# Scan and expert block in one kernel: masked logs as the moving operand, and one weight shift of four units on another engine

## The chip, the cores and the metric

One core of one Trainium2 chip runs the whole program. The metric is the device time of one execution in microseconds (us). The median of three runs of the kernel before is 324.29 us, the lowest 323.87 us. The execution that was profiled took 324.25 us, and its trace covers a span of 322.6 us.

## The reference, cut to what matters

A decayed scan over 4 batches, 8 heads and 768 positions, in chunks, and behind it a two-layer block over all 3072 tokens:

```
log_a = np.log(np.clip(a, 1e-06, 1.0))
cum = np.cumsum(la, axis=-1)
L = np.exp(cum[:, :, :, None] - cum[:, :, None, :]) * causal
y[:, :, sl] = einsum(CB * L, xc) + einsum(Cc, state) * decay_to_i
state = decay_full * state + np.sum(Bx, axis=2)
...
h = x @ w_in
g = h - np.tanh(h)
return (g @ w_out).astype(np.float32)
```

The weights `w_in` (256 x 2048) and `w_out` (2048 x 256) arrive as 64-bit floats. The chip gets them as pairs of 32-bit words, and has to make 32-bit floats of them itself.

## The kernel before, in words

**Scan.** The 768 positions of a batch are cut into chunks of Q = 112, and the chunks of the four batches take turns: numbers 0 to 3 are the first chunk of each batch, 4 to 7 the second, and so on to 27. A chunk stands in 128 partitions, of which the first N = 16 hold the carried state and the other 112 the positions. For each chunk the kernel makes `att` (the products of B and C, on PE into PSUM), `lt` (the exponentials of sums of logs, by ACT), their product (DVE), a triangular cut of it (POOL, except in the first four chunks), and `y` (PE). ACT copies of `y` into rows 0 to 15 of a later chunk's `x` hand on the state, `z0` and `z1` doing this for the first four chunks. There is one buffer for `att` from chunk 4 on, so the next `att` may be written only when DVE has read the one before.

**First four chunks.** Their exponents are made by `first_tile`. For each half of the heads (i = 0, 1), `fn_k` (L443) lets POOL write four 128x128 tiles `lm`, one for each head: the log of partition j, where j lies behind column m, and zero elsewhere. `fn_f` first adds the table `never` through the unit matrix `eye` (L448), which puts a large negative number where the causal mask is zero, and then multiplies (L451) each head's `lm` as weights with the triangle `upto` moving, 112 columns a head. ACT takes the exponential (`fn_x`, L467), DVE multiplies with `att` (`fn_m`, L471). The tiles `cp` share two PSUM buffers (`ph`), the `lm` three SBUF buffers.

**Chunks 4 to 9** are made from running sums that went out to DRAM and came back (`lt_c`, `rt_c`; `chunk_a`: `att` L507 and L512, exponential L516, product L520, cut L532), later ones in `chunk_l` (L550).

**Weights.** There are eight units, 512 words of each layer in each unit. `conv(u)` turns the words into a 32-bit float and then into a rounded part `wh` and a remainder `wl`. Its steps are: ACT scales the high words (`fn0`, L325, tile `wv`); DVE shifts the low words right by 29 (`fn1`, L330, tile `wm`, one buffer); DVE clamps (`fn2`, L335), joins (`fn3`, L338) and adds the sign (`fn4`, L345, which for the second layer of units 0 and 1 writes `wf` instead); ACT rounds to `wh` (L349); DVE subtracts to `wl` (L352). Units 0 and 1 do this in two halves of 512, the others in one piece of 1024.

**Expert block.** Tokens stand in eight tiles of 256 (tiles 0 to 3) and 512 columns. `mm1` multiplies with the first layer into `ph` (L756 for tile 0 with the unsplit floats of units 0 and 1, L763 with three products of parts), `act` computes tanh (ACT, L794) and the difference (DVE, L798) and splits the result into `gh` (ACT, L802) and `gl` (DVE, L808), `mm2` multiplies with the second layer into `o` (L834 with `wf`, L844 with parts). Tiles 0 to 3 go first, while the first chunks and the first weights are still being made; `keep` (L872) copies their `o`.

**The order of the work.** Nothing is issued in the order of the code. Each `op(engine, cost, function, r, w)` records an operation with a cost in us, and `Order.search` makes 16 list schedules with a random jitter drawn from `SEED`, keeps the shortest by its own costs, and issues the instructions of every engine and of the DMA queue SP in that order. On the chip each engine then takes its instructions strictly in that order. The costs, the engine named in an `op` and `SEED` therefore set the whole order.

Of the kernel before, what the change touches and what calls it, by code (L numbers as in the profile page):

```python
# [10 lines left out]
F32 = mybir.dt.float32  # L11
# [4 lines left out]
AF = mybir.ActivationFunctionType  # L16
ALU = mybir.AluOpType
# [3 lines left out]
P = 128  # L21
NB, H, S, D, N = 4, 8, 768, 32, 16
# [4 lines left out]
Q = P - N  # L27
# [7 lines left out]
BANK = 512  # L35
# [23 lines left out]
PLAIN = 1  # L59
FIRST = 4  # L60
URGE, WHOLE = 3.0, 2


class Order:
# [1 line left out]


    DMA_LATENCY, SEM, SEM_PE, RATE, FLIGHT = 0.8, 0.15, 0.28, 0.32e6, 8
    ROUNDS, JITTER, SEED, EARLY, LOOK = 16, 0.3, 266, 8.0, 0.5

    def __init__(self):
        self.ops, self.urge = [], []
# [4 lines left out]
    def slot(self, tag, bufs):  # L77
        k = self.count[tag] = self.count.get(tag, -1) + 1
        self.fresh[f"{tag}#{k}"] = tag, f"{tag}#{k - bufs}"
        return f"{tag}#{k}"  # L80
# [142 lines left out]
def tile_ssm_moe(ctx: ExitStack, tc: tile.TileContext, a, x, bn, bc, wts, out):  # L223
    nc = tc.nc
# [5 lines left out]
    p3 = ctx.enter_context(tc.tile_pool(name="p3", bufs=3))  # L230
# [6 lines left out]
    upto = head.tile([P, P], F32, name="upto")  # L237
    after = head.tile([P, P], F32, name="after")

    op = Order()  # L240
    slot = op.slot
    grp = {g: {} for g in range(NG)}
    chs = {c: {} for c in range(NCK)}
    raws, gs, po, n_po, obs, misc = {}, {}, {}, {}, {}, {}

    chunks = {t: [k for k in range(NCK) if (START[t] <= OFF[k] or t == 0) and OFF[k] < START[t + 1]] for t in range(NT)}
    wv, wm, pts, n_pt = {}, {}, {}, {}
# [63 lines left out]
    def part(s, v):  # L311
        return v[:, s].bitcast(F32)

    def conv(u, halves=False):
        raw, n = raws[u, 0], 2 if halves else 1
        n_v, n_m = op.pieces(slot("wv", 2), n), op.pieces(slot("wm", 1), n)
        convs[u] = n_v[0]

        def whole(s):
            return u < WHOLE and s.start == 1  # L320

        def fn0(s):
            if s.start == 0:
                wv[u] = p2.tile([P, 2, 512], U32, tag="wv", name=f"wv{u}")
            nc.scalar.activation(part(s, wv[u]), raws[u][:, s, :, 1].bitcast(F32), AF.Copy, scale=REBIAS)  # L325

        def fn1(s):
            if s.start == 0:
                wm[u] = p1.tile([P, 2, 512], U32, tag="wm", name=f"wm{u}")
            nc.vector.tensor_scalar(out=wm[u][:, s], in0=raws[u][:, s, :, 0], scalar1=29, scalar2=None,  # L330
                                    op0=ALU.logical_shift_right)

        def fn2(s):
            vf = part(s, wv[u])
            nc.vector.tensor_scalar(out=vf, in0=vf, scalar1=-CLAMP, scalar2=CLAMP, op0=ALU.max, op1=ALU.min)  # L335

        def fn3(s):
            nc.vector.scalar_tensor_tensor(out=wm[u][:, s], in0=wv[u][:, s], scalar=3, in1=wm[u][:, s],  # L338
                                           op0=ALU.logical_shift_left, op1=ALU.bitwise_or)

        def fn4(s):
            to = wv[u][:, s]
            if whole(s):
                to = wf[:, u : u + 1].bitcast(U32)
            nc.vector.scalar_tensor_tensor(out=to, in0=wv[u][:, s], scalar=0x80000000, in1=wm[u][:, s],  # L345
                                           op0=ALU.bitwise_and, op1=ALU.bitwise_or)

        def hi(s):
            nc.scalar.copy(wh[:, u, s], part(s, wv[u]).rearrange("p i (k c) -> p i k c", k=2))  # L349

        def lo(s):
            nc.vector.tensor_tensor(out=wl[:, u, s], in0=part(s, wv[u]).rearrange("p i (k c) -> p i k c", k=2),  # L352
                                    in1=wh[:, u, s].bitcast(F32), op=ALU.subtract)

        for i in range(n):
            s, k = (slice(i, i + 1), 0.6) if halves else (slice(0, 2), 1.0)
            n_r = raw[s]
            n_h, n_l = [f"wh{u}.{j}" for j in range(2)][s], [f"wl{u}.{j}" for j in range(2)][s]
            op("ACT", 1.0 * k, lambda s=s: fn0(s), r=n_r, w=[n_v[i]])
            op("DVE", 0.7 * k, lambda s=s: fn1(s), r=n_r, w=[n_m[i]])  # L360
            op("DVE", 0.65 * k, lambda s=s: fn2(s), w=[n_v[i]])
            op("DVE", 1.2 * k, lambda s=s: fn3(s), r=[n_v[i]], w=[n_m[i]])
            if whole(s):
                op("DVE", 1.2 * k, lambda s=s: fn4(s), r=[n_m[i], n_v[i]], w=[f"wf{u}"])
                continue
            op("DVE", 1.2 * k, lambda s=s: fn4(s), r=[n_m[i]], w=[n_v[i]])
            op("ACT", 1.05 * k, lambda s=s: hi(s), r=[n_v[i]], w=n_h)
            op("DVE", 1.2 * k, lambda s=s: lo(s), r=[n_v[i]] + n_h, w=n_l)
# [66 lines left out]
    def first_tile():  # L435


        n_a = op.pieces(slot("att", 1), 2)
        place = {}

        def fn_k(ck, i):
            chs[ck]["k", i] = p3.tile([P, BANK], F32, tag="g", name=f"lm{ck}_{i}").rearrange("p (h m) -> p h m", h=4)
            nc.gpsimd.affine_select(out=chs[ck]["k", i], in_=la[:, 4 * i : 4 * i + 4, ck : ck + 1].broadcast_to([P, 4, P]),  # L443
                                    pattern=[[0, 4], [-1, P]], compare_op=ALU.is_gt, fill=0.0, base=0, channel_multiplier=1)

        def fn_f(ck, i):
            f = chs[ck]["f", i] = ps_h.tile([P, 4, P], F32, tag="ph", name=f"cp{ck}_{i}")
            nc.tensor.matmul(out=f[:, :, 0:Q], lhsT=eye, rhs=never.unsqueeze(1).broadcast_to([P, 4, Q]),  # L448
                             start=True, stop=False, skip_group_check=True)
            for h in range(4):  # L450
                nc.tensor.matmul(out=f[:, h, 0:Q], lhsT=chs[ck]["k", i][:, h], rhs=upto[:, N:P], start=False, stop=h == 3,  # L451
                                 skip_group_check=True)

        def fn_p(ck):
            if ck == 0:
                att = ps_a.tile([P, 4, 4 * P], F32, tag="att", name="att0")
                place[0] = att[:, :, 0 : 4 * Q].rearrange("p i (k q) -> p i k q", k=4)
            bb, cc = operands(ck)
            for i in range(4):
                r = slice(32 * i, 32 * i + 2 * N)  # L460
                nc.tensor.matmul(out=place[0][:, i, 2 * (ck % 2) : 2 * (ck % 2) + 2], lhsT=bb[r], rhs=cc[r],  # L461
                                 start=True, stop=True)

        def fn_x(ck, i):
            if i == 0:
                chs[ck]["l"] = p3.tile([P, H, P], F32, tag="lt", name=f"lt{ck}", bufs=NL)[:, :, N:P]
            nc.scalar.activation(chs[ck]["l"][:, 4 * i : 4 * i + 4], chs[ck]["f", i][:, :, 0:Q], AF.Exp)  # L467

        def fn_m(ck, i):
            lt = chs[ck]["l"][:, 4 * i : 4 * i + 4].rearrange("p (i w) q -> p i w q", i=2)  # L470
            nc.vector.tensor_tensor(out=lt, in0=place[0][:, 2 * i : 2 * i + 2, 2 * (ck % 2) : 2 * (ck % 2) + 2],  # L471
                                    in1=lt, op=ALU.mult)

        for ck in range(FIRST):
            urge = URGE if ck < len(chunks[0]) else 0.0
            k = chs[ck]
            k["n_l"] = op.pieces(slot("lt", NL), 2)
            if ck % CPG == 0:
                prep(ck // CPG)
            for i in range(2):  # L480
                n_f, n_k = slot("ph", NPH), slot("g", 3)
                op("POOL", 0.7, lambda ck=ck, i=i: fn_k(ck, i), r=["la"], w=[n_k], urge=urge)
                op("PE", 1.14, lambda ck=ck, i=i: fn_f(ck, i), r=[n_k, "upto", "never"], w=[n_f])
                op("ACT", 0.52, lambda ck=ck, i=i: fn_x(ck, i), r=[n_f, "tab"], w=[k["n_l"][i]], urge=urge)
                if i == 0:
                    op("PE", 0.59, lambda ck=ck: fn_p(ck), r=[grp[ck // CPG]["n_bc"]], w=[n_a[ck % 2]])
                op("DVE", 0.6, lambda ck=ck, i=i: fn_m(ck, i), r=[n_a[ck % 2]], w=[k["n_l"][i]], urge=urge)
            if ck == 0:
                for i in range(4):
                    for j in range(2):  # L490
                        op("SP", 0.7, lambda i=i, j=j: get_parts(i, j), r=["cum3"], w=[("lt_c", "rt_c")[j]], dma=KB // 2)
            chunk_y(ck)
# [428 lines left out]
    la = cp.tile([P, H, NCK], F32, name="la")  # L921
# [5 lines left out]
    never = cp.tile([P, P], BF16, name="never")[:, 0:Q]  # L927
# [144 lines left out]
    for i in range(2):  # L1072
# [4 lines left out]
       r=[n_pq2], w=["wdec"])  # L1077

    first_tile()
    for G in range(-(-FIRST // CPG), 2):  # L1080
        prep(G)
    conv(0, True)
    group(2)
    state(0)
# [30 lines left out]
    for ck in at_:  # L1115
        if OFF[ck + 1] > START[NSW + 1]:
            for t in range(NSW):
                if COL[NSW + 1] <= COL[t] < COL[NSW + 1] + OFF[ck + 1] - START[NSW + 1]:
                    g = max(g for g, step in enumerate(steps) if t in OF[step[0]])
# [16 lines left out]
    for g in range(len(steps) + LAG):  # L1136
        if g < len(steps):
            t, f, _ = steps[g]
# [61 lines left out]
```

## Time and profile before

| | |
|---|---|
| profiled execution | 324.25 us |
| its span | 322.6 us |
| outside the span | 1.65 us |
| PE busy | 313.7 us (97%) |
| DVE busy | 215.3 us (67%) |
| ACT busy | 210.3 us (65%) |
| POOL busy | 60.6 us (19%) |
| last matmul begins, last stores are issued from | 318.35 us, 318.71 us |

PE is the matmul engine and PEld its weight loads, DVE the vector engine, ACT the scalar engine, POOL the engine of the masks, SP the queue that issues nearly all DMAs. Busy times of PE are made of pipelined matmuls, of which the trace shows two records for each product of 32-bit floats. In a row of the timeline the first number is the start, the second the length, and the bracket at its end tells how long the engine was idle before and what ended that. In the list of waits stand engine, line, what was waited for, total us, times and the longest.

### The profile page before, as it was taken

The numbers are of one execution on the slowest core, as the hardware profiler recorded it, in microseconds if no ns is written. First come the engines' busy times: TensorE is split into PE (matmuls) and PEld (weight loads), VectorE is DVE, ScalarE is ACT, GpSimd is POOL, SyncE is SP. The second block draws the span as 40 slices with busy tenths as digits, with TensorE's granted clock in tenths as the row PEclk, the third lists the DMA queues.
The fourth block names the chain that finished last, engine by engine and source line by source line (L and its number), as shares of the span: only waits on it lengthen the run. The fifth ranks groups of instructions, "written<-read, shape, count | busy, mean of one in ns | idle before, by whom it ended". The sixth has DMA issues, their size and how long they took to land.

```text
span 322.6 us, 5757 instructions
## 1 busy us (share of the span) xinstructions
PE 313.7 (97%) x2160; PEld 255.3 (79%) x2160; DVE 215.3 (67%) x314; ACT 210.3 (65%) x471; POOL 60.6 (19%) x94
## 2 busy tenths in 40 slices
PE   8997999999999999999999999999999999999995
PEld 7765888788888878787878887888878788888883
DVE  6978997898888867457563864664765645645552
ACT  6568888477687888575945854966868544534451
POOL 8604424003122514402300400111102000000000
PEclk9999999999999999999999999999999999999999
DMA  6679557539433149280606005005420000100001
GB/s 205 195 238 325 173 162 307 183 94 346 89 65 66 30 98 272 48 241 5 205 0 207 16 0 209 1 2 226 168 61 0 2 0 0 68 1 0 2 0 65
DMA packets 15451, 35.27 MB, mean 109 GB/s; under 512 B 2464, under 2 KB 4416, under 8 KB 15424
## 3 DMA queue, kind: packets, MB, share of 16 engines
q1 hardware_dynamic: 13696, 31.76, 29.4%
q0 software_dynamic: 1728, 3.15, 5.7%
q8 instruction: 17, 0.28, 0.4%
q14 instruction: 10, 0.08, 0.1%
HBM read 28.32 MB, written 3.43 MB: 98 GB/s over the span
## 4 chain that ended last, share of the span: by engine, by line
PE 91%; DVE 5%; ACT 2%; issue 1%
PE ph L763 39%; PE o L844 38%; PE o L834 3%; PE y L704 3%; PE att L678 3%; PE y L637 1%; PE warm L1003 1%; DVE lt L471 1%; ACT lt L550 1%; DVE lt L520 1%; DVE wv L345 1%; PE att L461 1%; PE cp L451 1%; ACT lt L516 1%; DVE wm L338 1%
## 5 line engine op out<-in xcount | busy, mean ns | idle before, releaser
L798 DVE TENSOR_TENSOR g<-ph,g 128x512 f32<-128x512 f32 x96 | 65.7, 688 | 52.1 <-ACT g L794 52.0
L794 ACT ACTIVATE g<-ph 128x512 f32<-128x512 f32 x96 | 57.3, 598 | 48.7 <-PE ph L763 47.8
L808 DVE TENSOR_TENSOR gl<-g,gh 128x512 fp32r<-128x512 f32 x88 | 62.7, 715 | 31.0 <-ACT gh L802 29.5
L763 PE MATMUL ph<-xh,wh 128*128 128x512 f32 (+1 forms) x200 | 76.0, 382 | 0.0
L763 PE MATMUL ph<-xh,wl 128*128 128x512 f32 (+1 forms) x200 | 74.8, 377 | 0.0
L802 ACT CAST gh<-g 128x512 fp32r<-128x512 f32 x88 | 54.4, 620 | 28.3 <-DVE g L798 26.4
L844 PE MATMUL o<-gh,wh 128*128 128x512 f32 x176 | 69.2, 393 | 0.0
L844 PE MATMUL o<-gl,wh 128*128 128x512 f32 x176 | 68.5, 389 | 0.0
L844 PE MATMUL o<-gh,wl 128*128 128x512 f32 x176 | 68.5, 389 | 0.0
L763 PE MATMUL ph<-xl,wh 128*128 128x512 f32 (+1 forms) x200 | 59.0, 376 | 0.0
L532 POOL TENSOR_SCALAR_AFFINE_SELECT lt<-lt 128x896 f32<-128x896 f32 (+1 forms) x24 | 23.3, 969 | 128.4 <-ACT lt L550 118.3
L763 PEld LDWEIGHTS ph<-xh,wh 128*128 128x128 f32 x200 | 37.6, 188 | 7.6 <-issue 0.6
L763 PEld LDWEIGHTS ph<-xh,wl 128*128 128x128 f32 x200 | 37.6, 188 | 6.8
L763 PEld LDWEIGHTS ph<-xl,wh 128*128 128x128 f32 x200 | 36.7, 188 | 7.0
L550 ACT ACTIVATE lt<-lt,ncum 128x112 f32<-128x112 f32 (+1 forms) x144 | 41.7, 375 | 0.0
L844 PEld LDWEIGHTS o<-gh,wh 128*128 128x128 f32 x176 | 33.0, 188 | 7.8 <-issue 0.8
L844 PEld LDWEIGHTS o<-gl,wh 128*128 128x128 f32 x176 | 33.0, 188 | 6.9
L844 PEld LDWEIGHTS o<-gh,wl 128*128 128x128 f32 x176 | 33.1, 188 | 6.7
L684 DVE TENSOR_TENSOR lt<-att,lt 128x896 f32<-128x896 f32 (+1 forms) x18 | 18.9, 1052 | 0.0
L888 POOL DMA_DIRECT2D pt<-part x12 | 11.1, 1023 | 41.1 <-ACT part L885 38.1
L834 PE MATMUL o<-g,wf 128*128 128x256 f32 x64 | 15.4, 384 | 1.4 <-ACT x L578 0.9
L605 ACT CAST xh<-y 128x224 fp32r<-128x224 f32 (+4 forms) x18 | 7.3, 413 | 13.1 <-DVE s L711 10.6
(97 smaller groups left out, 275.0 us busy)
## 6 DMA issues: line engine op xcount, KB each, us to landing
lt<-cumr SPq DMA_DIRECT2D x18, 512.0 KB
raw<-w_d SPq DMA_DIRECT2D x16, 512.0 KB
bc<-bc_d SPq DMA_DIRECT2D x14, 352.0 KB
x<-x_d SPq DMA_DIRECT2D x14, 256.0 KB
pt<-part POOLq DMA_DIRECT2D x12, 256.0 KB, 4.5
out_d<-ob SPq DMA_DIRECT2D x8, 256.0 KB
braw<-bn_d SPq DMA_DIRECT2D x14, 112.0 KB
out_d<-pt SPq DMA_DIRECT2D x4, 256.0 KB
```

The costliest lines, as they stand in the source:

```text
L532: nc.gpsimd.affine_select(out=k["l"][:, :, 0:q], in_=k["l"][:, :, 0:q], pattern=[[0, H], [1, q]], compare_op=ALU.is_ge, fill=0.0, base=N, ...
L550: nc.scalar.activation(k["l"][:, h, 0:q], k["l"][:, h, 0:q], AF.Exp, bias=ncum[:, h, ck : ck + 1])
L678: nc.tensor.matmul(out=a_[:, i], lhsT=bb[r], rhs=cc[r, :, 0 : qlen(ck)], start=True, stop=True)
L684: nc.vector.tensor_tensor(out=l, in0=chs[j]["a"], in1=l, op=ALU.mult)
L763: nc.tensor.matmul(out=ph[:, i * w : i * w + w], lhsT=w_[:, u, 0, k, j * P : (j + 1) * P], rhs=(xh, xl)[p][:, k, ts], start=p == 0 and k = ...
L794: nc.scalar.activation(g[:, 0:used], gs[t, f][0][:, 0:used], AF.Tanh)
L798: nc.vector.tensor_tensor(out=g, in0=ph, in1=g, op=ALU.subtract)
L802: nc.scalar.copy(gh[:, 0:used], gs[t, f][1][:, 0:used])
L808: nc.vector.tensor_tensor(out=gl[:, 0:used], in0=g[:, 0:used], in1=gh[:, 0:used].bitcast(F32), op=ALU.subtract)
L834: nc.tensor.matmul(out=po[t, seg][e], lhsT=wf[:, u, 256 * j + e * P : 256 * j + (e + 1) * P], rhs=gs[t, f][1][:, i * w : i * w + w], start ...
L844: nc.tensor.matmul(out=po[t, seg][e], lhsT=w_[:, u, 1, j, e * P : (e + 1) * P], rhs=g[:, i * w : i * w + w], start=f == seg[0] and k == 0 ...
L888: op("POOL", 1.0, lambda e=e: nc.gpsimd.dma_start(out=pts[m][:, e], in_=obs[t, e], accum_op=ALU.add), r=[name, n_pt[2 * m], n_pt[2 * m + 1 ...
```

## The change

`fn_k` now writes one tile of 4 heads x 112 columns (not 4 x 128): the log of partition j where position q has reached j, and zero elsewhere. `fn_f` multiplies it in one matmul of 448 moving columns with the constant triangle `after` as weights, where four matmuls of 112 columns with four different weights stood. The sums are the same. The shift by 29 of units 0 to 3 (`EASED`) becomes a scaled ACT copy that rounds to an unsigned integer; units 4 to 7 keep the DVE shift. The costs of these three operations in the table of the order are new, and `SEED` is another one, so every engine's order is another one as well.

```
-    ROUNDS, JITTER, SEED, EARLY, LOOK = 16, 0.3, 266, 8.0, 0.5
+    ROUNDS, JITTER, SEED, EARLY, LOOK = 16, 0.3, 39, 8.0, 0.5
...
+EASED = 0, 1, 2, 3
...
+            if u in EASED:
+                nc.scalar.activation(wm[u][:, s], raws[u][:, s, :, 0], AF.Copy, scale=2.0 ** -29, bias=-0.5 - 2.0 ** -20)
+                return
...
-            op("DVE", 0.7 * k, lambda s=s: fn1(s), r=n_r, w=[n_m[i]])
+            op(*(("ACT", 1.02 * k) if u in EASED else ("DVE", 0.7 * k)), lambda s=s: fn1(s), r=n_r, w=[n_m[i]])
...
-            chs[ck]["k", i] = p3.tile([P, BANK], F32, tag="g", name=f"lm{ck}_{i}").rearrange("p (h m) -> p h m", h=4)
-            nc.gpsimd.affine_select(out=chs[ck]["k", i], in_=la[:, 4 * i : 4 * i + 4, ck : ck + 1].broadcast_to([P, 4, P]),
-                                    pattern=[[0, 4], [-1, P]], compare_op=ALU.is_gt, fill=0.0, base=0, channel_multiplier=1)
+            lm = p3.tile([P, BANK], F32, tag="g", name=f"lm{ck}_{i}")
+            k = chs[ck]["k", i] = lm[:, 0 : 4 * Q].rearrange("p (h q) -> p h q", h=4)
+            nc.gpsimd.affine_select(out=k, in_=la[:, 4 * i : 4 * i + 4, ck : ck + 1].broadcast_to([P, 4, Q]),
+                                    pattern=[[0, 4], [1, Q]], compare_op=ALU.is_ge, fill=0.0, base=N, channel_multiplier=-1)
...
-            for h in range(4):
-                nc.tensor.matmul(out=f[:, h, 0:Q], lhsT=chs[ck]["k", i][:, h], rhs=upto[:, N:P], start=False, stop=h == 3,
-                                 skip_group_check=True)
+            nc.tensor.matmul(out=f[:, :, 0:Q], lhsT=after, rhs=chs[ck]["k", i], start=False, stop=True, skip_group_check=True)
...
-                op("POOL", 0.7, lambda ck=ck, i=i: fn_k(ck, i), r=["la"], w=[n_k], urge=urge)
-                op("PE", 1.14, lambda ck=ck, i=i: fn_f(ck, i), r=[n_k, "upto", "never"], w=[n_f])
+                op("POOL", 0.65, lambda ck=ck, i=i: fn_k(ck, i), r=["la"], w=[n_k], urge=urge)
+                op("PE", 0.98, lambda ck=ck, i=i: fn_f(ck, i), r=[n_k, "after", "never"], w=[n_f])
```

**Three places where the order moves.** First SP's queue, which issues the DMAs, at the start of the program: `bc0` to `bc2` are the B and C operands of the pairs of chunks 0 and 1, 2 and 3, 4 and 5; `x` is the input of a pair, `raw` the words of a unit in two halves, `cum3` the running sums on their way out. Before:

```order
L265 DMA bc0_136<-bc_d 128x704
L265 DMA bc1_138<-bc_d 128x704
L296 DMA raw0_147<-w_d 128x1024
L277 DMA x0_156<-x_d 128x512
L277 DMA x1_158<-x_d 128x512
L265 DMA bc2_160<-bc_d 128x704
L286 DMA braw0_106<-bn_d 112x256
L1051 DMA cum3_115<-parts_111 112x3x128 x2
L296 DMA raw0_147<-w_d 128x1024
```

Now:

```order
L266 DMA bc0_150<-bc_d 128x704
L278 DMA x0_159<-x_d 128x512
L287 DMA braw0_106<-bn_d 112x256
L297 DMA raw0_176<-w_d 128x1024
L1054 DMA cum3_115<-parts_111 112x3x128 x2
L297 DMA raw0_176<-w_d 128x1024
L266 DMA bc1_208<-bc_d 128x704
L278 DMA x1_217<-x_d 128x512
L266 DMA bc2_219<-bc_d 128x704
```

`bc1`, `x1` and `bc2` stood ahead of the running sums, and now stand behind them and behind the second half of unit 0.

Second PE, from the last `y` of the first four chunks to the `y` of chunk 4 (`att4`, `att5` are the chunks' products, `ph0_0` the first `mm1`, `z0` and `z1` states). Before:

```order
L512 MATMUL att4_365<-bc2_160 128x224 x4
L756 MATMUL ph0_0_377<-xf_93,wv0_206 128x256 x4
L572 MATMUL z0_391<-x0_156,bw0_256 16x32 x16
...
L512 MATMUL att5_416<-bc2_160 128x224 x4
L572 MATMUL z1_435<-x1_158,bw1_279 16x32 x16
L637 MATMUL y4_453<-lt4_383,x2_314 32x112 x8
```

Now:

```order
L759 MATMUL ph0_0_336<-xf_93,wv0_231 128x256 x4
...
L515 MATMUL att4_348<-bc2_219 128x224 x4
L575 MATMUL z0_360<-x0_159,bw0_266 16x32 x16
L575 MATMUL z1_391<-x1_217,bw1_343 16x32 x16
...
L515 MATMUL att5_412<-bc2_219 128x224 x4
L640 MATMUL y4_429<-lt4_377,x2_307 32x112 x8
```

The first `mm1` stood between `att4` and `att5`, and now stands ahead of both; the two states follow each other.

Third DVE, where unit 3 is made (`wm3`, `wv3`, and `wl` from `wv3`) among the products `lt10`, `lt11`, the differences `g` and unit 4. Before:

```order
L335 TENSOR_SCALAR wv3_658<-wv3_658 128x1024
L798 TENSOR_TENSOR g2_2_776<-ph2_2_747,g2_2_776 128x512
L338 SCALAR_TENSOR_TENSOR wm3_724<-wv3_658,wm3_724 128x1024
L345 SCALAR_TENSOR_TENSOR wv3_658<-wv3_658,wm3_724 128x1024
L608 TENSOR_TENSOR xl_92<-y9_797,xh_91 128x2x112
L684 TENSOR_TENSOR lt10_706<-att10_788,lt10_706 128x8x112
```

Now:

```order
L687 TENSOR_TENSOR lt11_710<-att10_745,lt11_710 128x8x112
L801 TENSOR_TENSOR g3_0_833<-ph3_0_805,g3_0_833 128x512
L339 TENSOR_SCALAR wv3_835<-wv3_835 128x1024
L801 TENSOR_TENSOR g3_2_839<-ph3_2_819,g3_2_839 128x512
L342 SCALAR_TENSOR_TENSOR wm3_842<-wv3_835,wm3_842 128x1024
L349 SCALAR_TENSOR_TENSOR wv3_835<-wv3_835,wm3_842 128x1024
L714 STREAM_TRANSPOSE s10_891<-y10_854 128x128
L611 TENSOR_TENSOR xl_92<-y10_854,xh_91 128x2x224
L334 TENSOR_SCALAR wm4_897<-raw4_802 128x1024
L339 TENSOR_SCALAR wv4_874<-wv4_874 128x1024
L801 TENSOR_TENSOR g8_4_893<-ph8_4_877,g8_4_893 128x512
L356 TENSOR_TENSOR wl_90<-wv3_835,wh_89 128x1024
```

Unit 3 was joined ahead of `lt10`, and now is joined behind `lt11` and behind the differences of tile 3.

## The prediction, on record before the kernel ran

> **What bounds the kernel now.** I read the page, then PE's busy time over one long stretch, then PE's list of waits, then the timelines of all engines from 4 to 66 us. The page:
>
> ```profile
> span 322.6 us, 5757 instructions
> PE 313.7 (97%) x2160; PEld 255.3 (79%) x2160; DVE 215.3 (67%) x314; ACT 210.3 (65%) x471; POOL 60.6 (19%) x94
> PE 91%; DVE 5%; ACT 2%; issue 1%
> ```
>
> and one stretch of PE (length, then busy us of PE):
>
> ```profile
> 64.50:318.50 254.00, 254.00 (x1418) 207.01 (x1417) 160.75 (x230) 165.22 (x367) 35.66 (x47) 1.00 0.27 80
> ```
>
> PE carries 91% of the chain that ended last, and from 64.5 us to the end it never waits, at a granted clock of 1.00. Behind PE only a tail is left. The change adds nothing to this work and takes nothing from it. So the time can move only by PE work that goes away, and by waits of PE before that stretch. All of these are in PE's own list:
>
> ```profile
> PE o L834 <- ACT x L578: 0.9, 1, 0.9
> PE z L572 <- POOL bc L395: 0.8, 1, 0.8
> PE att L507 <- DVE lt L520: 0.6, 1, 0.6
> PE o L834 <- DVE g L798: 0.5, 1, 0.5
> PE y L637 <- POOL lt L532: 0.5, 1, 0.5
> PE y L637 <- ACT xf L601: 0.5, 1, 0.5
> PE cp L448 <- ACT lt L467: 0.4, 1, 0.4
> PEld cp L451 <- POOL lm L443: 0.5, 1, 0.5
> PEld att L461 <- DVE lt L471: 0.6, 2, 0.3
> ```
>
> That is 4.2 us on PE and 1.1 us more that only its weight loads show. If every one went, the time would fall by 5.3 us, or 1.6%. A measurement of this kernel tells about 2% (6.5 us) from no change, so faster by that much is nearly closed.
>
> **The masked logs.** The first cp group and what surrounds it:
>
> ```profile
> 5.27 0.55 PE L1037 MATMUL pr<-la,upto 128*128 128x224 f32 x2
> 5.65 0.35 PE L448 MATMUL cp<-never,eye 128*128 128x448 bf16 x1
> 5.84 1.04 PE L451 MATMUL cp<-upto,lm 128*128 128x112 f32 x8
> 6.71 0.56 PE L1037 MATMUL pq<-la,after 128*128 128x224 f32 x2
> L443 POOL TENSOR_SCALAR_AFFINE_SELECT lm<-la x8: 627/880/1079, 4.6 to 12.9; 128x512 f32<-128x512 f32 x8
> ```
>
> From start to start a group takes 6.71 - 5.65 = 1.06 us. One 32-bit product of 224 moving columns takes 5.65 - 5.27 = 0.38 us, so 448 columns take 0.76 us; with the mask's 0.19 us (5.84 - 5.65) the new group takes 0.95 us. Eight groups save 8 x 0.11 = 0.9 us of PE. POOL writes 448 columns where it wrote 512: 0.63 us becomes about 0.55 us, hidden behind PE.
>
> **The shift.** Its rows of before (first 62 us; count, total us, mean ns), with the nearest rows for its ACT form, which reads the same words at the same stride:
>
> ```profile
> L330 DVE TENSOR_SCALAR wm<-raw 128x512 uint32<-128x512 uint32 x4 | 2.2, 556 | 0.0
> L330 DVE TENSOR_SCALAR wm<-raw 128x1024 uint32<-128x1024 uint32 x3 | 2.9, 954 | 0.1
> L325 ACT ACTIVATE wv<-raw 128x512 f32<-128x512 f32 x4 | 2.7, 687 | 2.5 <-DMA raw<-w_d 2.3
> L325 ACT ACTIVATE wv<-raw 128x1024 f32<-128x1024 f32 x3 | 3.5, 1166 | 0.0
> ```
>
> DVE loses 4 x 0.56 + 2 x 0.95 = 4.1 us, and ACT gains 4 x 0.69 + 2 x 1.17 = 5.1 us. The trace has no ACT copy from integers to integers. Its lower bound is the DVE row (0.56 and 0.95), its upper one twice the ACT row (1.37 and 2.33); I take the ACT row, which has the same reads. Neither engine bounds the time by its sum: what counts is where the six pieces stand.
>
> [...]
>
> **The start, walked in the new order.** PE begins the groups at 5.65 us as before. Eight groups (7.6), two att blocks (1.2) and the product pq (0.4) bring it to 14.85 us, where it wants the att of chunks 2 and 3. These need bc1, now issued behind the running sums and behind unit 0's second half. What that costs is in these rows:
>
> ```profile
> 9.77 0.50 SPq L296 DMA_DIRECT2D raw<-w_d  x1
> 14.74 0.69 ACT L325 ACTIVATE wv<-raw 128x512 f32<-128x512 f32 x1 [1.41 <-DMA raw<-w_d]
> 12.00:14.00 2.00, 1.90 (x20) 1.44 (x20) 1.82 (x4) 1.33 (x3) 1.82 (x3) 1.00 0.72 256
> ```
>
> That half was issued at 9.77 us and landed at 14.7, with the DMA engines moving 256 GB/s before that (the last row, 12 to 14 us). bc1's 352 KB come right behind it and take 1.4 us at that rate, so it lands at about 16.1 us, and POOL's copy (0.2) makes it 16.3. PE waits 1.5 us there, and while it does it makes no difference whether a cp group takes 0.95 us or, as the upper bound, still 1.06. Then both att blocks (1.2) and two y (0.95) end at 18.4; DVE's four products (L471, four halves in 2.3 us) end at 19.2, and the fourth y at 19.8. The first mm1 takes 1.9: att4 starts at 21.7 us. From here the rows are
>
> ```profile
> 20.56 0.28 PE L507 MATMUL att<-rt_c,lt_c 9*128 9x224 bf16 x4
> 21.16 1.99 PE L756 MATMUL ph<-xf,wv 128*128 128x256 f32 x8
> 21.31 0.92 ACT L516 ACTIVATE lt<-att 128x896 f32<-128x896 f32 x1 [0.26 <-PE att L512]
> 22.26 1.09 DVE L520 TENSOR_TENSOR lt<-att,lt 128x896 f32<-128x896 f32 x1 [0.79 <-ACT lt L516]
> 23.75 1.05 ACT L578 COPY x<-z 16x128 f32<-16x128 f32 x4
> 24.77 0.98 POOL L532 TENSOR_SCALAR_AFFINE_SELECT lt<-lt 128x896 f32<-128x896 f32 x1
> 24.78 1.51 DVE L345 SCALAR_TENSOR_TENSOR wv<-wv,wm 128x512 uint32<-128x512 uint32 x1
> 25.80 0.59 PE L637 MATMUL y<-lt,x 128*32 128x112 f32 x16 [0.48 <-POOL lt L532]
> 26.44 1.99 PE L756 MATMUL ph<-xf,wv 128*128 128x256 f32 x8
> ```
>
> Before, the mm1 of 1.99 us ran while ACT and DVE worked on att4. Now it is over before att4 starts. So after att4 (to 22.3) PE has only z0 (0.4), then waits: the exponential ends at 23.4, the product (0.1 + 1.1) at 24.6, the copies of z0 at 24.45, and z1 and att5 run to 25.55. POOL's cut makes y4 possible at 25.75. Before, it began at 25.80. **At y4 all is given back**: the 0.9 us of groups, and the waits that went, are spent on bc1 and under att4.
>
> Next is the second mm1 (26.44 before), which wants unit 1's first half. On ACT its two pieces now stand behind the copies of z0: 24.45 + 2 x 0.6 = 25.65. DVE's join and sign (0.7 each without POOL beside them) end at 27.1; in the trace the sign took 1.51 beside POOL's cut, which is over by then. So this mm1 starts at 27.2, **0.75 us late**.
>
> Behind it PE's blocks follow each other closely. Their lengths, from the chain:
>
> ```profile
> 33.77 1.62 PE ph L763 x12
> 35.39 1.73 PE o L834 x8
> ```
>
> With att blocks of 0.6 and y of chunks 5 to 9 at 0.65, PE wants the first o at 29.8 us, y5 at 31.5, att7 at 33.8, and the first o of tile 3 at 59.3. What they need is earlier. The copies of z1, behind unit 1's shift and the next exponential on ACT, end at 28.0, so the buffer of o is free. The product for y5 ends at 28.3, its cut at 29.4. The product for att7 ends at 32.0. The difference of tile 3 ends at 56.3, and ACT frees that o's buffer at 58.2. So the waits of the list on L578 (0.9), L520 (0.6) and g (0.5) go: **-2.0 us**. SP holds one more danger: it issues x4 only when z1 is done (25.0), with the second half of unit 1 behind it. At 4.9 us from issue to landing (9.77 to 14.74 above) that is there at 30.4; ACT wants it at 30.8. The ACT pieces added here (0.7, 1.2 and 1.2 us) lie in its gaps while PE works through 32 us.
>
> The last doubtful place is unit 3, first used by the third block of the wide tile 8. Before, its pieces stood early; the rows also show a join (L338) beside POOL and one alone:
>
> ```profile
> 54.71 0.69 DVE L330 TENSOR_SCALAR wm<-raw 128x1024 uint32<-128x1024 uint32 x1
> 58.67 1.22 DVE L352 TENSOR_TENSOR wl<-wv,wh 128x1024 fp32r<-128x1024 f32 x1
> 40.12 1.92 DVE L338 SCALAR_TENSOR_TENSOR wm<-wv,wm 128x1024 uint32<-128x1024 uint32 x1
> 49.85 1.22 DVE L338 SCALAR_TENSOR_TENSOR wm<-wv,wm 128x1024 uint32<-128x1024 uint32 x1
> ```
>
> Now ACT's shift follows the tanh of tile 3 and DVE has eight further pieces between it and the remainder. I find the remainder ready at 64.1 us and PE there at 64.3: no slack. I put 0.05 us for it.
>
> **Sum**: +0.75 - 2.0 + 0.05 = -1.2 us; the 0.9 us saved is inside it, spent earlier. From the profiled 324.25 us, which stands 0.04 under the median of the runs, I forecast **323.0 us**.
>
> **Rivals.** (a) *The start stays ahead.* If bc1 lands by 14.85 us, everything up to the second mm1 comes 1.1 us earlier. For it: bc0, x0 and braw0 leave the queue empty sooner. Against it: the half of unit 0 itself landed only at 14.7. Time: 324.25 - 1.2 - 1.1 = 321.95 us. (b) *Unit 3 is late, slower than before.* One place, PE's first block with unit 3, one mechanism: ACT's shift is queued behind tanh and exponentials, DVE's join and sign behind that, and a transpose, a split and unit 4 stand ahead of the remainder. Each us by which it ends after 64.3 is a us of the span, and from 1.25 us late the change loses. With the shift at its upper bound (2.33 for 1.17) and a join beside POOL (1.92 for 1.22) it is 1.9 us late: 324.25 - 1.25 + 1.9 = 324.9 us. For it: no slack. Against it: POOL has only a small copy there, and ACT reads the same words in L325 without such a stretch. (c) *The edits pay, the order does not*: the new waits match the old ones, and only the 0.9 us of groups against the 1.0 us that ACT is dearer remain: 324.35 us. For it: three waits in a row at the start, none of them hidden. Against it: the waits of the old order that I let go have 1.1 to 3 us of slack in the new one.
>
> **How the numbers follow.** Forecast 0.45, (a) 0.2, (b) 0.15, (c) 0.2. The range goes from 321.4 us, rival (a) with half a us more where POOL and DVE no longer meet, to 325.0 us, which holds rival (b) and the upper bound of the shift at units 1 and 3 together (324.25 - 1.2 + 0.7 + 1.2 = 324.95). I leave 0.2 outside. All four cases lie within 2% (317.8 to 330.7): same 0.96, faster 0.01, slower 0.03, the last for a cast on ACT that costs far more than its upper bound.
>
> **What would show it.** Right: cp groups of 0.95 us with one matmul of 448 columns; PE waiting for bc or the DVE product before the att of chunks 2 and 3, near 15 us; PE waits of about 2 us between z0 and att5; the second mm1 at 27 us; no wait from there to 64 us; the 254.00 us of solid PE unchanged; ACT's shifts at 0.69 and 1.17 us. Wrong: att of chunks 2 and 3 before 15.2 us (rival a), PE waiting at the first block with unit 3 (rival b), waits that add to 5 us (rival c), or any wait behind 66 us.

## The result, and the profile after

The changed kernel takes 325.99 us (median of 6 runs, 325.15 to 326.51), the kernel before, beside it, 324.07. One of the six runs of the kernel before took 631.2 us; the ratio leaves it out, and the median of its other five runs is 323.87 us. The ratio is 1.0066, 95% interval 1.005 to 1.0082: **slower by 0.66%**, some 2 us. The forecast was 323.0 us, faster by 0.4%, with a range to 325.0: wrong in its sign, and outside its range. The profiled execution took 325.34 us.

The page of the changed kernel, with the row of the granted clock:

```profile
span 323.6 us, 5658 instructions
PE 314.5 (97%) x2112; PEld 251.9 (78%) x2112; DVE 210.9 (65%) x308; ACT 213.0 (66%) x477; POOL 62.2 (19%) x94
PEclk9997999999999999999999999999999999999999
PE 94%; DVE 2%; ACT 2%; issue 1%; POOL 0%; DVEq 0%; ACTq 0%
```

The span is 1.0 us longer, although 48 matmul records are gone, and PE is busy for 0.8 us more. The fourth slice of the clock row, a 7 among nines, is where to look: slices are 8.1 us long, so it is the time from 24.3 to 32.4 us. Next PE's list of waits, to be held against the nine rows shown of before (the wait at the program's start, 0.8 us in both kernels, is left out of both):

```profile
PE z L575 <- ACT x L581: 1.7, 1, 1.7
PE att L681 <- DVE lt L687: 1.2, 1, 1.2
PE ph L759 <- DVE wv L349: 1.1, 1, 1.1
PE y L640 <- DVE lt L474: 0.2, 1, 0.2
PE y L640 <- POOL lt L535: 0.2, 1, 0.2
```

The waits on the copies of z (0.9), on the product for att7 (0.6) and on `g` (0.5) are gone, as forecast. There is a wait of 1.7 us between the two states, forecast as about 2, one of 1.1 us ahead of the second `mm1`, and one of 1.2 us on `att` that was not forecast. PE's timeline places them:

```profile
5.93 0.35 PE L453 MATMUL cp<-never,eye 128*128 128x448 bf16 x1
6.12 0.92 PE L455 MATMUL cp<-lm,after 128*128 128x448 f32 x2
6.87 0.35 PE L453 MATMUL cp<-never,eye 128*128 128x448 bf16 x1
...
15.44 1.04 PE L464 MATMUL att<-bc 32*128 32x224 f32 x16
...
23.77 0.43 PE L575 MATMUL z<-x,bw 128*16 128x32 f32 x32 [1.68 <-ACT x L581]
24.97 0.59 PE L640 MATMUL y<-lt,x 128*32 128x112 f32 x16 [0.16 <-POOL lt L535]
26.77 3.39 PE L759 MATMUL ph<-xf,wv 128*128 128x256 f32 x8 [1.09 <-DVE wv L349]
30.09 0.28 PE L510 MATMUL att<-rt_c,lt_c 9*128 9x224 bf16 x4
...
58.48 1.04 PE L681 MATMUL att<-bc 32*128 32x224 f32 x16 [1.21 <-DVE lt L687]
```

The eight matmuls of the second `mm1` took 3.39 us; the same eight took 1.99 us before (26.44, shown above). The busy times by stretch (PE, PEld, DVE, ACT, POOL, then the granted clock, the DMA share and GB/s) give the reason:

```profile
22.00:24.00 2.00, 0.33 (x44) 0.26 (x32) 1.76 (x3) 1.97 (x6) 0.71 (x2) 1.00 0.69 192
24.00:26.00 2.00, 1.51 (x71) 0.99 (x55) 1.60 (x2) 1.93 (x5) 1.26 (x2) 1.00 0.49 126
26.00:28.00 2.00, 1.23 (x3) 1.05 (x4) 1.98 (x3) 1.93 (x7) 0.21 (x1) 0.56 0.98 350
28.00:30.00 2.00, 2.00 (x6) 1.38 (x5) 0.73 (x2) 0.46 (x3) 1.52 (x2) 0.59 1.04 327
...
26.00:27.00 1.00, 0.23 (x1) 0.23 (x2) 0.98 (x2) 0.96 (x4) 0.00 (x0) 0.61 0.99 322
27.00:28.00 1.00, 1.00 (x3) 0.82 (x4) 1.00 (x2) 0.96 (x4) 0.21 (x1) 0.50 0.98 379
28.00:29.00 1.00, 1.00 (x3) 0.78 (x3) 0.73 (x2) 0.46 (x3) 1.00 (x1) 0.50 1.00 297
29.00:30.00 1.00, 1.00 (x4) 0.60 (x2) 0.00 (x0) 0.00 (x0) 0.52 (x2) 0.68 1.09 356
...
66.00:319.00 253.00, 253.00 (x1415) 206.40 (x1414) 162.26 (x231) 162.47 (x365) 36.95 (x47) 1.00 0.29 85
```

PE was busy for 0.33 of the 2 us from 22 to 24, and from 26 to 30 us the granted clock is 0.56 and 0.59. In stretches of 1 us it is exactly 0.50 inside, with an edge at each end: counted as half speed, 0.61, 0.50, 0.50 and 0.68 make 3.4 us, from 26.2 to 29.6 us. The block that came right behind the waits ran at half speed nearly to its end. The long stretch to the end (last row) is as solid as before.

So the ledger of the profiled execution, start to start on PE, is: second `mm1` begins 26.77 - 26.44 = 0.33 us later (0.28 of it is there already at the first cp group, 5.93 against 5.65; over all the kernels profiled here, with the same matmuls ahead of it, this group begins anywhere from 5.17 to 6.85 us); it takes 30.09 - 26.77 = 3.32 us where at a clock of 1.00 it takes 1.93 (measured below), +1.39; the old waits are gone, -1.92 (0.86, 0.56 and 0.50); the new wait for `att` is +1.21. The sum is +1.01 us, and the spans differ by 1.0. The medians differ by more (1.9 us): half of the changed kernel's runs have a lower mean clock still (0.989 where the profiled one has 0.994) and are about 1 us longer. As an estimate, 3.4 us at half speed take 0.005 off the mean over 323.6 us, so 0.989 would be twice that time; no profile caught such a run.

### The profile page after: what moved, and what is told of

The parts are those of the page before. It is cut to its first block, busy times and chain, and to the rows that moved or that the text cites. A ratio compares the mean times of both kernels' runs of the same rounds, so it can differ in the third digit from the quotient of the medians.

```text
span 323.6 us, 5658 instructions
## 1 busy us (share of the span) xinstructions
PE 314.5 (97%) x2112; PEld 251.9 (78%) x2112; DVE 210.9 (65%) x308; ACT 213.0 (66%) x477; POOL 62.2 (19%) x94
## 4 chain that ended last, share of the span: by engine, by line
PE 94%; DVE 2%; ACT 2%; issue 1%; POOL 0%; DVEq 0%; ACTq 0%
PE ph L766 39%; PE o L847 37%; PE o L837 4%; PE y L707 3%; PE att L681 3%; PE cp L455 2%; PE ph L759 2%; PE warm L1006 1%; PE y L640 1%; PE att L464 1%; ACT lt L553 1%; PE cp L453 1%; DVE lt L474 1%; PE att L515 0%; PE pr L1035 0%
## 5 line engine op out<-in xcount | busy, mean ns | idle before, releaser
L811 DVE TENSOR_TENSOR gl<-g,gh 128x512 fp32r<-128x512 f32 x88 | 64.1, 731 | 36.4 <-ACT gh L805 35.5
L535 POOL TENSOR_SCALAR_AFFINE_SELECT lt<-lt 128x896 f32<-128x896 f32 (+1 forms) x24 | 25.2, 1051 | 131.0 <-ACT lt L553 114.3
L611 DVE TENSOR_TENSOR xl<-y,xh 128x224 fp32r<-128x224 f32 (+4 forms) x18 | 8.4, 469 | 9.0 <-ACT x L653 4.7
```

The costliest lines, as they stand in the source:

```text
L535: nc.gpsimd.affine_select(out=k["l"][:, :, 0:q], in_=k["l"][:, :, 0:q], pattern=[[0, H], [1, q]], compare_op=ALU.is_ge, fill=0.0, base=N, ...
L811: nc.vector.tensor_tensor(out=gl[:, 0:used], in0=g[:, 0:used], in1=gh[:, 0:used].bitcast(F32), op=ALU.subtract)
```

## The experiments

Each kernel was timed beside the kernel before, whose medians were 324.06, 324.26 and 324.02 us in the three groups. The theories were: *the edits themselves cost more than they save*; *the new order loses it by the granted clock*; *the new order loses it by the wait at 58 us*.

### The edits without the order

The first kernel is before with the new masked logs alone (`fn_k` as in the change, and the lines below); all costs in the table, the seed and thus the order stay as they were.

```
-            for h in range(4):
-                nc.tensor.matmul(out=f[:, h, 0:Q], lhsT=chs[ck]["k", i][:, h], rhs=upto[:, N:P], start=False, stop=h == 3,
-                                 skip_group_check=True)
+            nc.tensor.matmul(out=f[:, :, 0:Q], lhsT=after, rhs=chs[ck]["k", i], start=False, stop=True, skip_group_check=True)
```

> The kernel before with the new masked logs alone; the order is planned with the costs and the seed of before, so every queue stands as before. Theory (the order, through the granted clock and one new wait, makes the change slower; the edits themselves do not): cp groups of 0.95 us instead of 1.06, between 0 and 0.9 us of it reaching the end, clock 1.00, 323.2 to 324.1 us. Rival (the new product is itself the loss): 325 us or more.

Measured: 323.95 us, ratio 1.0001 (0.9981 to 1.0021).

The second is before with ACT's shift alone, still recorded as DVE's 0.7 in the table, so that each piece stands where it stood among the others:

```
+            if u in (0, 1, 2, 3):
+                nc.scalar.activation(wm[u][:, s], raws[u][:, s, :, 0], AF.Copy, scale=2.0 ** -29, bias=-0.5 - 2.0 ** -20)
+                return
```

> The kernel before with the shift of units 0 to 3 on ACT alone, in the order of before (the ACT copy stands where the plan had the DVE shift). Theory (the order makes the change slower, not the edits): 323 to 324.6 us, since DVE loses 4.1 us in a stretch where it is nearly always busy and ACT gains 4.6 us where it has gaps. Rival (ScalarE is the dearer engine for this and its queue holds up tanh and the exponentials): 325 us or more, with PE waiting for g or lt in 20 to 60 us.

Measured: 324.38 us, ratio 1.0015 (1.0 to 1.0031).

The third has both edits in the old order.

> Both edits in the order of before. Theory (order): 322.5 to 324.3 us, not slower than before, granted clock 1.00 throughout. Rival (edits): as slow as the change, near 326 us.

Measured: 324.17 us, ratio 1.001 (0.9991 to 1.0028). The edits alone neither gain nor lose anything clear of the spread of the runs. What the change loses, **its order loses**. Why the 0.9 us of PE work saved in the first groups does not show as a gain is read from the second kernel's waits, with the shift alone,

```profile
PE z L575 <- POOL lt L535: 1.3, 1, 1.3
PE cp L451 <- ACT lt L470: 0.6, 1, 0.6
```

and the third's, with both edits:

```profile
PE z L574 <- POOL lt L534: 1.3, 1, 1.3
PE cp L452 <- ACT lt L469: 0.8, 1, 0.8
PE att L463 <- DVE lt L473: 0.5, 2, 0.2
```

The wait of 1.3 us on a state (0.8 before) comes with ACT's shift. With the new groups added, PE waits 0.2 us longer for the exponentials (`cp`) and 0.5 us for DVE's products (`att`), which the second kernel's list does not have at all; all of PE's waits from 4 us on add up to 4.5 us there and 3.5 us without the groups. So the time that the groups save stands again as wait, in good part within the groups themselves.

### Filling the waits

The next kernel is the change with constant matmuls in the two waits: seven behind `z0`, into an `o` buffer that is not in use yet, and five ahead of the second `mm1`, into the tile that it then overwrites. They depend on nothing that is late and compute nothing that is used.

```
+    def fill(v, n):
+        one = nc.const_aps.tensor(1.0, (P, P), F32)
+        for i in range(n):
+            nc.tensor.matmul(out=v[0:32, i % 4, :], lhsT=one[:, 0:32], rhs=one, start=True, stop=True)
...
+            if G == 0:
+                fill(ps_o.tile([P, 4, P], F32, tag="po1", name="fill"), 7)
...
+            if plain(t, f) and f == 2:
+                fill(ph.rearrange("p (i q) -> p i q", i=4), 5)
```

> The change with two runs of constant matmuls added on PE, 7 behind z0 (1.5 us) and 5 ahead of the second first-layer block (1.1 us), where PE waits; nothing reads them. Theory (these waits let the granted clock fall to half, and the block then takes 3.3 us instead of 1.9): the block takes 1.9 us, granted clock 1.00 from 20 to 30 us, 1.3 us less than the change, 324.6 us or less. Rival (the block is slow because its operands arrive beside a full DMA queue and busy DVE and ACT): the block still takes over 3 us, and the time stays at 326 us or grows by what the added matmuls hold up.

Measured: 323.78 us, ratio 0.9991 (0.9977 to 1.0005), 2.2 us under the change. PE's timeline of this kernel:

```profile
21.63 1.72 PE L568 MATMUL fill<-const-float32-1.0 128*32 128x128 f32 x14
23.48 0.43 PE L580 MATMUL z<-x,bw 128*16 128x32 f32 x32
...
25.20 1.27 PE L568 MATMUL ph<-const-float32-1.0 128*32 128x128 f32 x10
26.48 1.99 PE L768 MATMUL ph<-xf,wv 128*128 128x256 f32 x8
28.41 0.27 PE L510 MATMUL att<-rt_c,lt_c 9*128 9x224 bf16 x4
```

The states and the second `mm1` start no later for the work in front of them (`z0` begins at 21.38 us here and at 21.67 in the change, with `z1` 2.10 us and the `mm1` 5.10 us behind it in both), and the `mm1` takes 28.41 - 26.48 = 1.93 us, at a granted clock of 1.00 in every us from 22 to 30. PE does more work in all, and the kernel is faster: what cost these 2.2 us was not the waits but **the clock behind them**.

Which of the two waits does it? The two fills apart (the same code, one call left out):

> The change with only the 5 constant matmuls ahead of the second first-layer block (1.1 us); the wait of 1.7 us behind z0 stays empty. If the clock falls by how little PE does over the whole stretch from 22 to 26.8 us, part of it is kept: the block takes 1.9 to 2.6 us and the time is 324 to 325 us. If it falls by the one longest wait, nothing changes for the block: it takes 3.3 us, 325.9 us.

Measured, with the fill ahead of the `mm1` alone: 324.52 us, ratio 1.0013 (0.9995 to 1.003). The runs split in two: six at a mean clock of 1.00 with 323.58 to 324.13 us, six at 0.992 to 0.995 with 324.92 to 325.91 us, by their medians 1.4 us apart. The profiled one is of the second kind:

```profile
22.00:24.00 2.00, 0.33 (x40) 0.30 (x32) 1.73 (x3) 1.97 (x6) 0.75 (x2) 1.00 0.73 229
24.00:26.00 2.00, 1.98 (x68) 1.42 (x52) 1.62 (x3) 1.81 (x4) 1.22 (x2) 0.62 0.42 106
26.00:28.00 2.00, 2.00 (x20) 1.48 (x10) 1.94 (x3) 1.92 (x8) 0.25 (x1) 0.52 0.73 178
28.00:30.00 2.00, 2.00 (x14) 1.46 (x13) 0.82 (x2) 0.56 (x3) 1.28 (x1) 1.00 1.02 346
```

Behind the wait of 1.68 us alone the clock falls to 0.62 and 0.52 although PE is busy all the time by then, so the end of `att`, the `y` of chunk 4 and the fill run slowly in place of the `mm1`. Counted as half speed, 0.62 and 0.52 make 3.4 us again, from 24.5 to 27.9 us.

> The change with only the 7 constant matmuls behind z0 (1.5 us); the wait of 1.1 us ahead of the block stays empty. If the longest wait decides, or if the activity over the whole stretch does, the granted clock stays at 1.00, the block takes 1.9 us and the time is 323.8 to 324.2 us. If the last wait ahead of the block decides, it still takes 3.3 us, 325.9 us.

Measured, with the fill behind `z0` alone: 323.94 us, ratio 0.9992 (0.9982 to 1.0002), all 12 runs at a clock of 1.00. The wait of 1.09 us is still there, and the block behind it runs at full speed:

```profile
26.96 1.99 PE L766 MATMUL ph<-xf,wv 128*128 128x256 f32 x8 [1.09 <-DVE wv L349]
```

So the wait of 1.09 us alone did no harm in any of 12 runs, and that of 1.68 us did it in 6 of 12. Two more kernels ask whether a wait must be long in one piece, or whether short ones add up. The first puts three constant matmuls behind `z0`, the second one, where there were seven:

```
-                fill(ps_o.tile([P, 4, P], F32, tag="po1", name="fill"), 7)
+                fill(ps_o.tile([P, 4, P], F32, tag="po1", name="fill"), 3)
```

> The change with 3 constant matmuls (about 0.74 us) behind z0 where the kernel with 7 filled the whole wait; the wait of 1.09 us ahead of the second mm1 stays. So PE has two waits of about 0.95 and 1.09 us, 2.04 us in all, with 2 us of work between. Theory one (a single long wait lowers the granted clock, and the longest that did not is 1.3 us in the old order with the shift on ACT): clock 1.00 from 20 to 30 us in every run, second mm1 1.9 us start to start, 323.9 us. Theory two (the sum of the waits over some us counts, and 2.0 us is more than the 1.6 us that the kernel before had there): granted clock about 0.5 at 26 to 29 us in most runs, second mm1 over 2.5 us, 325 us or more. Either way z1 itself begins at 23.77 us.

> The same with one constant matmul (about 0.25 us): waits of about 1.43 and 1.09 us. Theory one puts the length at which a wait lowers the clock between 1.3 us (the old order with the shift on ACT, clock 1.00) and 1.68 us (the change, 0.5 to 0.6): this run tells on which side 1.43 us lies, 323.9 us if above the limit is not reached and 325.2 us or more if it is, or a mixture of the two over its runs. Theory two: as the change itself, clock 0.5 to 0.6 at 26 to 30 us in all runs, 325.5 to 326 us.

Measured: with three 325.52 us (10 runs, 324.04 to 326.63), ratio 1.0044 (1.0021 to 1.0067); with one 325.9 us (5 runs, 323.43 to 326.23), ratio 1.0042 (1.0003 to 1.008). The first theory fell: no wait is longer than 1.09 us with three, and six of ten runs are slow. The second came nearer (most runs with three, but four of five and not all with one; the kernel before has 1.26 us there, not the 1.6 us of the text). With three, four runs have a mean clock of 0.999 or 1.00 (324.04 to 324.76 us) and six of 0.989 or 0.994 (325.25 to 326.63 us); its profiled execution, one of the four, has waits of 1.03, 0.31 and 1.09 us and a clock of 1.00:

```profile
22.00:24.00 2.00, 1.16 (x42) 0.80 (x38) 1.96 (x3) 1.97 (x7) 0.11 (x1) 1.00 0.82 251
24.00:26.00 2.00, 1.51 (x70) 1.14 (x74) 1.46 (x3) 1.97 (x4) 1.82 (x3) 1.00 0.50 142
26.00:28.00 2.00, 0.91 (x26) 0.73 (x16) 1.97 (x3) 1.95 (x7) 0.00 (x0) 1.00 0.95 350
```

With one, four of five runs have a lowered clock, and the profiled execution shows it:

```profile
22.00:24.00 2.00, 0.57 (x37) 0.30 (x34) 1.91 (x3) 1.96 (x7) 0.64 (x1) 1.00 0.56 173
24.00:26.00 2.00, 1.74 (x76) 1.25 (x76) 1.47 (x3) 1.94 (x4) 1.33 (x2) 1.00 0.45 122
26.00:28.00 2.00, 0.96 (x2) 0.84 (x3) 1.97 (x4) 1.93 (x8) 0.00 (x0) 0.75 0.97 368
28.00:30.00 2.00, 2.00 (x6) 1.57 (x5) 1.00 (x2) 0.72 (x4) 1.43 (x2) 0.50 1.09 342
```

All kernels together, with the waits that the timeline of the profiled execution shows on PE from 22 to 27 us, the most idle time of PE that any 3.4 us between 4 and 66 us hold there, and the runs whose mean clock was 0.995 or less (the last experiments are told below). The 3.4 us are the length of the lowered stretch above, 26.2 to 29.6 us; that idle time counts over just this length is the author's estimate, and not shown:

| kernel | waits, us | sum, us | most in 3.4 us | runs with a lowered clock |
|---|---|---|---|---|
| change, both waits filled | 0.16 | 0.16 | 1.21 | 0 of 12 |
| the same with the late cut | 0.16 | 0.16 | 0.22 | 0 of 6 |
| before with the masked logs | 0.78, 0.41 | 1.19 | 1.19 | 3 of 12 |
| before | 0.78, 0.48 | 1.26 | 1.42 | 1 of 78 |
| change, filled behind `z0` with seven | 0.17, 1.09 | 1.26 | 1.26 | 0 of 12 |
| before with ACT's shift | 1.33 | 1.33 | 1.33 | 0 of 12 |
| before with both edits | 1.33 | 1.33 | 1.33 | 3 of 12 |
| change, filled ahead of the `mm1` | 1.68 | 1.68 | 1.68 | 6 of 12 |
| change, filled with three | 1.03, 0.31, 1.09 | 2.43 | 1.67 | 6 of 10 |
| change, filled with one | 1.47, 0.16, 1.09 | 2.72 | 1.66 | 4 of 5 |
| change | 1.68, 0.16, 1.09 | 2.93 | 1.84 | 6 of 6 |
| change with the late cut | 1.68, 0.16, 1.09 | 2.93 | 1.84 | 12 of 12 |

Where no 3.4 us hold more than 1.42 us of idle time, 7 of 144 runs have a lowered clock; from 1.66 us on, 34 of 45. The longest wait does not decide: 1.09 us went with none of 12 runs and with six of ten. Whether the sum or the share of some 3.4 us decides, the table alone does not say. The profiles speak for the second: in all four that show a lowered clock (the change, the change with the late cut, filled ahead of the `mm1`, filled with one) the 3.4 us right ahead of the fall hold 1.66 to 1.68 us of idle time. That this is a limit is not shown: the profile with three holds 1.67 us and kept a clock of 1.00. Two reservations: the kernels with seven behind `z0` and with the fill ahead ran on one chip and those with three and one on another (on which the kernel before kept its clock in 14 of 14 runs); and two rows do not fit, before with the masked logs and with both edits. For both a clock of 1.00 had been expected, and of each 3 of 12 runs had 0.995 or less (medians of these 325.46 and 325.64 us). No profile caught one of them, so where the clock fell there is open. The clock row may also miss something at the start: in the profile with the masked logs the product of the first cp group took 1.70 us at 7.22 us, where the next one took 0.92, with a granted clock of 1.00 on record.

### The wait at 58 us

`att` of chunk 12 wants the buffer that DVE's product frees. The chain in front of it, from the timelines of ACT, POOL and DVE in the change:

```profile
53.71 2.34 ACT L553 ACTIVATE lt<-lt,ncum 128x112 f32<-128x112 f32 x8
56.12 0.99 POOL L535 TENSOR_SCALAR_AFFINE_SELECT lt<-lt 128x896 f32<-128x896 f32 x1 [3.07 <-ACT lt L553]
57.14 1.09 DVE L687 TENSOR_TENSOR lt<-att,lt 128x896 f32<-128x896 f32 x1 [1.91 <-POOL lt L535]
```

For these chunks the cut comes ahead of the product, and DVE sat idle for 1.91 us until the cut was done. The next kernel is the change with this one cut recorded behind its product; it makes the same triangle zero.

```
+LATE = 11,
...
-        op("POOL", 1.1, lambda: cut(ck), w=n_l)
+        op("POOL", 1.1, lambda: None if ck in LATE else cut(ck), w=n_l)
...
+            if j in LATE:
+                cut(j)
```

> The change with the triangular cut of chunk 11 issued behind its product with att instead of ahead of it (the same output; every other instruction stands as in the change). Theory (the wait of 1.2 us before att12 comes from exponential, cut and product of chunk 11 in a row, with only the product needed for att12's buffer): that wait falls to 0.2 us or less and the time by about 1.0, to 325.0 us. Rival (the wait covers another: unit 3 is just in time behind it): PE waits about as long a few us later, at the first block with unit 3 or at the pair's y, and the time stays near 326 us.

Measured: 325.16 us, ratio 1.0033 (1.0022 to 1.0045), 0.8 us under the change; all 12 runs still with a clock of 0.987 to 0.995, as the waits at 22 to 27 us are untouched. Its timeline:

```profile
56.03 1.09 DVE L688 TENSOR_TENSOR lt<-att,lt 128x896 f32<-128x896 f32 x1 [0.86 <-ACT lt L554]
...
57.38 1.04 PE L682 MATMUL att<-bc 32*128 32x224 f32 x16 [0.16 <-PE ph L769]
```

The product starts 1.1 us earlier, and PE's wait of 1.21 us is 0.16.

### Both

> The change with both runs of constant matmuls and the late cut. Theory (two separate losses that add): 1.0 us under the filled kernel and 3.2 under the change, 322.8 us, faster than before by 0.4%. Rival (unit 3 is next): 323.7 us, no better than the filled kernel.

Measured: 323.05 us (6 runs, 322.62 to 323.37), ratio 0.9963 (0.995 to 0.9976): faster than both kernels, by 0.37% under the one before. The two losses are separate and add up: 2.2 us from the fill, 0.8 from the cut, and 2.9 with both (325.99 - 323.05). What is left on PE's list from 4 us on:

```profile
PE y L648 <- DVE lt L475: 0.2, 1, 0.2
PE y L648 <- POOL lt L536: 0.2, 1, 0.2
PE att L689 <- PE ph L778: 0.2, 1, 0.2
```

With both losses mended, the changed order comes to the time that the prediction had worked out without them: 323.0 forecast, 323.05 measured. That it agrees so closely is in part luck, since the start had been priced higher than it came.

## Why the prediction was wrong

**The cp groups: right.** 0.95 us forecast from start to start, 6.87 - 5.93 = 0.94 measured; the matmul pair takes 0.75 of it.

**ACT's shift: right.** 0.69 and 1.17 us were taken from the rows of the other ACT pieces. The group of these shifts (shortest, median, longest in ns):

```profile
L332 ACT ACTIVATE wm<-raw x6: 659/672/1156, 11.6 to 58.1; 128x512 uint32<-128x512 uint32 x4, 128x1024 uint32<-128x1024 uint32 x2
```

The shift on ACT alone, in the old order, costs 0.15%, with 0 at the edge of its interval.

**The start: priced too high.** The `att` of chunks 2 and 3 came at 15.44 us (forecast 16.3), the `y` of chunk 4 at 24.97 (25.75), the second `mm1` 0.33 us late and not 0.75, and of the 0.33 us 0.28 were there before the first group. The forecast wait of 1.5 us for `bc1` is in no row of PE's list. Unit 0's second half landed at 14.2 us and not 14.7, and `bc1` 0.9 us behind it (15.09, where POOL's copy starts) and not 1.4. So rival (a), the start that stays ahead, came true in good part, though the `att` did not come before 15.2 us.

**The old waits: right.** 2.0 us forecast, 1.92 gone.

**The second `mm1`: the step that failed first.** The prediction forecast waits of PE of about 2 us there, priced them by the time at which the next block starts, and then let that block run for 1.9 us as ever. "At a granted clock of 1.00" was read from the stretch behind 64 us, and taken to hold at 27 us, behind more idle time than PE had had there before. That block took 3.32 us: +1.39 in the profiled execution, some 2.2 us by the medians with and without the fill. The two waits, the first forecast in words and the second by its times, had a price of their own behind them.

In rows of 1 us the lowered clock reads 0.50 (two rows in the change, three with one constant matmul), with a row between 0.50 and 1.00 at the edges, and counted as half speed the lowered stretch is 3.4 us long in each of the four profiles that show one. The mean clock was 0.995 or less with one wait of 1.68 us in 6 of 12 runs, and with gaps of at most 1.09 us that stood close together in 6 of 10. What sets the moment of the fall, and why one kernel keeps its clock in some runs and not in others, no run here shows.

**"No wait from there to 64 us": the second step that failed.** The recorded walk goes from the `att` of chunk 7 to the first `o` of tile 3, and does not name the `att` of chunk 12: it put nothing there, and gave no reason. From chunk 10 on the cut stands ahead of the product, which ended at 58.2 us. Before, the same `att` stood behind an `o` block that is 1.9 us long, and so began at 59.13 us, when DVE's product was over (57.07 and 1.08 us); in the new order it stands ahead of the `o` blocks, and nothing covers the chain. +1.21 us, of which mending the cut gave back 0.8.

**Unit 3: no wait.** 0.05 us had been put down for it, and rival (b) had made it the place where the change loses. No row of PE's list names it. **Rival (c)**, that the new waits match the old ones, was nearest in kind (324.35 us), and had no price for the clock either.

In sum: -1.2 forecast; -0.42 for the start, +0.08 and -0.05 for small terms, +1.39 for the clock and +1.21 for `att` make it +1.01.

## What to carry to other kernels

A new order is not only as good as the sum of its waits: where the clock of an engine falls behind idle time, as TensorE's did here (to 0.50, with 1.66 to 1.68 us of idle time in the 3.4 us ahead), several waits close together can be paid twice, once as idle time and once in the block behind them (3.32 us for 1.93), so each stretch of the walk (3.4 us here) wants its sum of idle time beside it, held against the stretch of the old order with the highest sum that kept its clock (1.84 us in the change, 1.42 before). Where such a wait cannot be removed, constant matmuls into a tile that is not in use yet are worth a try: here the mean clock was 0.997 or more in all 12 runs with them, and they cost nothing on the path (the `mm1` 5.10 us behind `z0` with and without them). And when an order is walked by hand, each chain must be walked in the sequence that its own code path records, above all where a block that had covered the chain now stands behind it.

## What the runs showed of the hardware that was not expected

- Behind 1.66 to 1.68 us of idle time within 3.4 us, in one piece or with matmuls in between, TensorE's granted clock fell to 0.50 for 3.4 us in each of four profiles (a fifth, with 1.67 us, kept 1.00), and the mean clock was 0.995 or less in 34 of 45 runs of five kernels (6 of 12 with one wait of 1.68 us, 18 of 18 where both waits of the change stood unfilled); behind waits of 0.17 and 1.09 us it was so in none of 12.
- The lowered clock began behind the idle time: with the fill ahead of the `mm1` at 24.5 us, 0.8 us after the wait had ended and with PE at work, and it stayed although PE was busy throughout; in the change at 26.2 us, 2.5 us after the longest wait had ended and in the middle of the wait ahead of the `mm1`.
- The ACT copies from 32-bit integers to 32-bit integers, with a scale and a bias, took about as long as those from such words to floats: 0.66 to 0.68 us for 512 words (0.69 before for the float), 1.14 and 1.16 us for 1024 (1.17).
